# Decay sums as two float32r products, casts on ScalarE and a product on VectorE, in a fused RWKV-6 and max-out MLP kernel

## Chip, cores and metric

One core of one Trainium2 chip. The time is the device time of one execution in microseconds (us), given as the median of a kernel's runs. The profiled span is some 1.7 us shorter than the time of the same run. A run is called slow when it lies over 1.5% above the fastest of the same kernel; slow runs are left out of every ratio. A ratio is the mean time of one kernel's fast runs over that of the kernel before in the same rounds on the same chip, so it is not quite the ratio of the medians quoted beside it. Where two experiments are compared with each other, the difference of their ratios is taken, times 170.5 us (the median of the kernel before).

## The reference, cut to what matters

```python
# B=4 sequences, H=8 heads, S=768 steps, D=48; float32 in and out
state = 0
for t in range(S):                       # RWKV-6 recurrence
    y[t]  = r[t] @ (state + outer(u*k[t], v[t]))
    state = w[t][:, None]*state + outer(k[t], v[t])      # w in 0.80..0.95
x  = y as (3072 tokens, 384)
h1 = x @ w1;  h2 = x @ w2                # 384 x 1024 each
out = maximum(h1, h2) @ w_out            # 1024 x 384
```

The kernel works in 12 units: unit `i` is a chunk of 128 steps of two sequences. In a chunk the decay becomes a running sum of `ln w`, made on TensorE by a triangular matrix of ones (`ex`), and its exponentials scale r and k (`rp`, `kp`). The maximum is written as (h1+h2)/2 + |h1-h2|/2, so that the MLP needs one large product with w1-w2 (`H`, whose result is `g_p`) and one with half the sum of both already multiplied by w_out.

## The kernel before: the parts that matter

Every engine runs its instructions strictly in the order in which a long hand-made list, `ORDER`, names them. A token is an operation, a unit and at times a sequence: `ex.3.1` is the decay sum of unit 3, sequence 1. In the comments, SBUF and PSUM are the core's two on-chip memories; TensorE's results land in PSUM.

```python
ORDER = """
ldw.0 ldw.1 ldk.0 ldu ldr.0 ldw12.2 ldv.0 ldw12.0 lw.0 ex.0.0 incl.0.0 aex.0.0 ...
... Y.0.1 aex.1.1 incl.1.1 ldwo YO.0.1 row.1 ldv.1 ...        # some 900 tokens, cut
"""
...
def ldwo():                                           # w_out, on GpSimd's queue
    nc.gpsimd.dma_start(out=wo_sb, in_=moe_w_out.rearrange("(o p) n -> p o n", p=C))
def lw(i):                                            # ScalarE: ln w, float32
    x = work.tile([C, NB, H, D], F32, tag="lw", name="lw")
    nc.scalar.activation(x, st["w", i], AF.Ln)
def ex(i, b):                                         # TensorE: the decay sum, float32
    ex_p = ps.tile([C, HD], F32, tag="ex", name="ex_p")
    nc.tensor.matmul(ex_p, triU, flat(st["lw", i][:, b]))
def incl(i, b):                                       # VectorE
    nc.vector.tensor_add(flat(st["incl", i][:, b]), st["ex", i, b], flat(st["lw", i][:, b]))
def rp(i):                                            # VectorE, two SBUF inputs
    nc.vector.tensor_mul(rps[i % 2][:, :, :, 0:D], st["r", i], st["Aex", i])
def kp(i):                                            # VectorE, two SBUF inputs
    nc.vector.tensor_mul(kps[i % 2][:, :, :, 0:D], st["k", i], st["Ainv", i])
def ku(i):                                            # GpSimd: k*u
    nc.gpsimd.tensor_mul(x, st["k", i]..., u_b...)
def rku(i):                                           # GpSimd: k*u*r
    nc.gpsimd.tensor_mul(st["ku", i], st["r", i]..., st["ku", i])
def bv(i):                                            # GpSimd: v times the sum of k*u*r
    nc.gpsimd.tensor_mul(x..., st["v", i]..., st["dg", i]...)
def vb(i):                                            # GpSimd: v in bf16
    nc.gpsimd.tensor_copy(x, st["v", i])
def TO(i, b):                                         # transposed rp, kp out of PSUM
    if b == 0: nc.scalar.copy(rkT, st.pop(("tp", i, b)))
    else:      nc.vector.tensor_copy(rkT, st.pop(("tp", i, b)))
def sb(i):                                            # GpSimd: state in bf16
    for a in range(2): nc.gpsimd.tensor_copy(S_z[bp][rows, :, :, a, :], S_f[bp][rows])
...
with tc.manual_schedule():
    for step in ORDER.split():
        name, *at = step.split(".")
        ops[name](*(int(x) for x in at))
```

Of the kernel before, what the change touches and what calls it, by code (L numbers as in the profile page):

```python
# [8 lines left out]
F32 = mybir.dt.float32  # L9
BF16 = mybir.dt.bfloat16  # L10
# [6 lines left out]
ldw.0 ldw.1 ldk.0 ldu ldr.0 ldw12.2 ldv.0 ldw12.0 lw.0 ex.0.0 incl.0.0 aex.0.0 ex.0.1 incl.0.1 ainv.0 row.0  # L17
ldw.2 ldw12.1 ldr.1 ldk.1 ku.0 aex.0.1 kp.0 lw.1 ex.1.0 rp.0 rku.0 T.0.0 TO.0.0 wsum.2 aex.1.0 M.0.0 T.0.1
MO.0.0 TO.0.1 vb.0 dg.0 M.0.1 Y.0.0 wT.2 incl.1.0 bv.0 MO.0.1 ex.1.1 wdif.2 wsum.0 YO.0.0 lw.2 wdif.0 X.0.0
Y.0.1 aex.1.1 incl.1.1 ldwo YO.0.1 row.1 ldv.1 ldw.3 wt.0 wdif.1 ldk.2 X.0.1 ldr.2 wsum.1 ex.2.0 ldw.4 XO.0  # L20
wT.0 wTO.2 aex.2.0 ainv.1 wTO.0 H.0.0 incl.2.0 H.0.1 HO.0.0 rp.1 K.0 HO.0.1 H.0.2 kp.1 ku.1 wT.1 HO.0.2 ex.2.1
sa.0 T.1.0 wTO.1 H.0.3 rku.1 TO.1.0 incl.2.1 wp.0 wt.1 row.2 ldv.2 ldk.3 HO.0.3 ldr.3 T.1.1 wpO.0 dg.1 M.1.0
aex.2.1 vb.1 wp.2 MO.1.0 bv.1 K.1 wpO.2 wp.1 sa.1 lw.3 TO.1.1 ainv.2 Y.1.0 ex.3.0 YO.1.0 wpO.1 aex.3.0
incl.3.0 X.1.0 M.1.1 ku.2 wx.0 kp.2 O1.0.0 MO.1.1 O2.0.0 rku.2 ex.3.1 sm.0 OO.0.0 Y.1.1 rp.2 aex.3.1 O1.0.1
YO.1.1 sb.0 lw.4 T.2.0 incl.3.1 O2.0.1 dg.2 TO.2.0 row.3 ldw.5 wt.2 X.1.1 ldv.3 ex.4.0 ldr.4 ldk.4 ldw.6 XO.1
T.2.1 M.2.0 OO.0.1 bv.2 TO.2.1 H.1.0 aex.4.0 incl.4.0 H.1.1 HO.1.0 MO.2.0 ex.4.1 ainv.3 vb.2 H.1.2 HO.1.1 kp.3
wx.1 M.2.1 ku.3 HO.1.2 K.2 incl.4.1 Y.2.0 H.1.3 rp.3 wt.3 ldv.4 ldk.5 O1.1.0 row.4 st.0.0 HO.1.3 rku.3 ldr.5
YO.2.0 ainv.4 MO.2.1 T.3.0 O1.1.1 lw.5 sa.2 TO.3.0 sm.1 Y.2.1 dg.3 X.2.0 sb.1 O2.1.0 aex.4.1 T.3.1 YO.2.1
OO.1.0 M.3.0 TO.3.1 X.2.1 O2.1.1 vb.3 XO.2 MO.3.0 ex.5.0 OO.1.1 bv.3 H.2.0 wx.2 incl.5.0 aex.5.0 H.2.1 sm.2
HO.2.0 rp.4 ex.5.1 HO.2.1 ku.4 M.3.1 kp.4 aex.5.1 K.3 H.2.2 MO.3.1 H.2.3 HO.2.2 sb.2 T.4.0 Y.3.0 TO.4.0 O1.2.0  # L30
YO.3.0 sa.3 HO.2.3 Y.3.1 incl.5.1 vb.4 X.3.0 M.4.0 YO.3.1 row.5 ainv.5 st.0.1 T.4.1 ldv.5 ldw.7 MO.4.0 ldw.8
rku.4 ldr.6 ldk.6 O1.2.1 st.1.0 lw.6 kp.5 X.3.1 wt.4 O2.2.0 st.1.1 XO.3 ku.5 dg.4 O2.2.1 OO.2.0 ex.6.0 TO.4.1
Y.4.0 aex.6.0 incl.6.0 H.3.0 rp.5 rku.5 K.4 ex.6.1 sa.4 OO.2.1 T.5.0 incl.6.1 wx.3 HO.3.0 M.4.1 bv.4 H.3.1
TO.5.0 dg.5 row.6 ldv.6 wt.5 ldw.9 ldr.7 H.3.2 ldk.7 HO.3.1 MO.4.1 T.5.1 ainv.6 H.3.3 vb.5 sm.3 HO.3.2 M.5.0
YO.4.0 sb.3 K.5 lw.7 TO.5.1 O1.3.0 MO.5.0 aex.6.1 HO.3.3 Y.4.1 bv.5 ex.7.0 sa.5 lw.8 YO.4.1 M.5.1 O1.3.1
aex.7.0 incl.7.0 MO.5.1 Y.5.0 X.4.0 X.4.1 YO.5.0 ex.7.1 rp.6 O2.3.0 aex.7.1 XO.4 O2.3.1 incl.7.1 ku.6 kp.6
Y.5.1 OO.3.0 ex.8.0 row.7 wx.4 st.2.0 YO.5.1 st.2.1 ldk.8 H.4.0 ldv.7 ldr.8 rku.6 OO.3.1 T.6.0 incl.8.0 wt.6
st.3.0 HO.4.0 X.5.0 st.3.1 sm.4 H.4.1 TO.6.0 X.5.1 H.4.2 HO.4.1 dg.6 M.6.0 vb.6 HO.4.2 T.6.1 aex.8.0 MO.6.0
H.4.3 sb.4 XO.5 ex.8.1 HO.4.3 TO.6.1 H.5.0 incl.8.1 bv.6 H.5.1 HO.5.0 M.6.1 HO.5.1 H.5.2 MO.6.1 aex.8.1 Y.6.0
wx.5 HO.5.2 O1.4.0 ainv.7 YO.6.0 rp.7 lw.9 Y.6.1 O2.4.0 ku.7 kp.7 wt.7 ldw.10 ldv.8 ex.9.0 row.8 ldk.9 ldr.9  # L40
OO.4.0 sm.5 K.6 ainv.8 T.7.0 incl.9.0 st.4.0 rku.7 H.5.3 YO.6.1 TO.7.0 sa.6 O1.4.1 aex.9.0 HO.5.3 X.6.0 kp.8
sb.5 X.6.1 O2.4.1 XO.6 M.7.0 dg.7 OO.4.1 ex.9.1 ku.8 H.6.0 incl.9.1 H.6.1 MO.7.0 HO.6.0 T.7.1 aex.9.1 HO.6.1
H.6.2 vb.7 rp.8 H.6.3 HO.6.2 bv.7 Y.7.0 wx.6 TO.7.1 O1.5.0 wx.7 M.7.1 HO.6.3 rku.8 YO.7.0 K.7 T.8.0 MO.7.1
O1.5.1 TO.8.0 sm.6 O2.5.0 ainv.9 sa.7 sb.6 Y.7.1 sm.7 OO.5.0 X.7.0 M.8.0 YO.7.1 lw.10 T.8.1 dg.8 wt.8 O1.6.0
ldw.11 vb.8 ldk.10 ldv.9 ldr.10 row.9 st.4.1 TO.8.1 st.5.0 bv.8 X.7.1 MO.8.0 O2.5.1 XO.7 O2.6.0 OO.5.1 kp.9
M.8.1 st.5.1 sb.7 ex.10.0 Y.8.0 rp.9 H.7.0 K.8 ku.9 OO.6.0 incl.10.0 T.9.0 aex.10.0 YO.8.0 st.6.0 ldv.10 H.7.1
ldr.11 HO.7.0 ldk.11 MO.8.1 TO.9.0 ex.10.1 rku.9 H.7.2 HO.7.1 sa.8 Y.8.1 aex.10.1 M.9.0 HO.7.2 YO.8.1 T.9.1
incl.10.1 H.7.3 MO.9.0 ainv.10 X.8.0 X.8.1 O1.6.1 HO.7.3 kp.10 XO.8 O1.7.0 dg.9 vb.9 lw.11 O2.6.1 TO.9.1 bv.9
O2.7.0 rp.10 ex.11.0 M.9.1 incl.11.0 ku.10 K.9 OO.6.1 T.10.0 aex.11.0 st.6.1 ldv.11 Y.9.0 OO.7.0 H.8.0 TO.10.0
YO.9.0 st.7.0 wt.9 H.8.1 sa.9 rku.10 HO.8.0 MO.9.1 T.10.1 HO.8.1 H.8.2 TO.10.1 H.8.3 HO.8.2 ex.11.1 wx.8 vb.10  # L50
M.10.0 incl.11.1 aex.11.1 Y.9.1 dg.10 O1.7.1 ainv.11 YO.9.1 HO.8.3 bv.10 X.9.0 O2.7.1 rp.11 O1.8.0 OO.7.1 sm.8
st.7.1 kp.11 sb.8 X.9.1 O2.8.0 O1.8.1 MO.10.0 OO.8.0 XO.9 st.8.0 ku.11 T.11.0 M.10.1 TO.11.0 Y.10.0 MO.10.1
O2.8.1 rku.11 T.11.1 OO.8.1 YO.10.0 H.9.0 st.8.1 H.9.1 HO.9.0 Y.10.1 wx.9 HO.9.1 dg.11 H.9.2 X.10.0 YO.10.1
H.9.3 HO.9.2 bv.11 sm.9 M.11.0 HO.9.3 O1.9.0 MO.11.0 vb.11 O1.9.1 TO.11.1 sb.9 O2.9.0 X.10.1 M.11.1 OO.9.0
O2.9.1 XO.10 st.9.0 Y.11.0 OO.9.1 H.10.0 YO.11.0 st.9.1 H.10.1 MO.11.1 HO.10.0 X.11.0 HO.10.1 H.10.2 Y.11.1
HO.10.2 H.10.3 YO.11.1 O1.10.0 HO.10.3 X.11.1 O2.10.0 XO.11 O1.10.1 OO.10.0 st.10.0 O2.10.1 H.11.0 OO.10.1
st.10.1 H.11.1 HO.11.0 H.11.2 HO.11.1 H.11.3 HO.11.2 O1.11.0 HO.11.3 O2.11.0 O1.11.1 OO.11.0 st.11.0 O2.11.1
OO.11.1 st.11.1
# [4 lines left out]
def kernel(  # L63
# [12 lines left out]
    nc = tc.nc  # L76
# [25 lines left out]
    make_upper_triangular(nc, triU, val=1.0, diag=False)  # L102
    u_b = const.tile([C, HD], F32)

# [28 lines left out]
    w1f = const.tile([C, KO, d_ff], F32)  # L133
    w2f = const.tile([C, KO, d_ff], F32)

# [8 lines left out]


    def ldw12(ko):
        nc.sync.dma_start(out=w1f[:, ko, :], in_=moe_w1[ko * C:(ko + 1) * C, :])
        nc.sync.dma_start(out=w2f[:, ko, :], in_=moe_w2[ko * C:(ko + 1) * C, :])
# [7 lines left out]
    def wsum(ko):  # L156
        nc.gpsimd.tensor_add(ws_sb[:, ko, :], w1f[:, ko, :], w2f[:, ko, :])

    def wdif(ko):
        nc.vector.tensor_sub(wd_sb[:, ko, :], w1f[:, ko, :], w2f[:, ko, :])  # L160
# [21 lines left out]
    def ld(name, src):  # L182
        def fn(i):
            c, bp = units[i]
            x = inp.tile([C, NB, H, D], F32, tag=name, name=f"{name}t")
            nc.sync.dma_start(
                out=x, in_=src[bp * NB:(bp + 1) * NB, :, c * C:(c + 1) * C, :].rearrange("b h s d -> s b h d"))
            st[name, i] = x
        return fn

    def lw(i):
        x = work.tile([C, NB, H, D], F32, tag="lw", name="lw")
        nc.scalar.activation(x, st["w", i], AF.Ln)  # L193
        st["lw", i] = x

    def ex(i, b):
        ex_p = ps.tile([C, HD], F32, tag="ex", name="ex_p")
        nc.tensor.matmul(ex_p, triU, flat(st["lw", i][:, b]))  # L198
        st["ex", i, b] = ex_p
# [11 lines left out]
    def ainv(i):  # L211
        x = work.tile([C, NB, H, D], F32, tag="Ainv", name="Ainv")
        nc.scalar.activation(x, st["incl", i], AF.Exp, scale=-1.0)  # L213
        st["Ainv", i] = x
# [18 lines left out]
    def rp(i):  # L233
        nc.vector.tensor_mul(rps[i % 2][:, :, :, 0:D], st["r", i], st["Aex", i])  # L234

    def kp(i):
        nc.vector.tensor_mul(kps[i % 2][:, :, :, 0:D], st["k", i], st["Ainv", i])  # L237

    def ku(i):
        x = work.tile([C, NB, HD], F32, tag="ku", name="ku")  # L240
        nc.gpsimd.tensor_mul(x, st["k", i].rearrange("p b h d -> p b (h d)"),  # L241
                             u_b.unsqueeze(1).to_broadcast([C, NB, HD]))
        st["ku", i] = x

    def rku(i):
        nc.gpsimd.tensor_mul(st["ku", i], st["r", i].rearrange("p b h d -> p b (h d)"), st["ku", i])  # L246

    def dg(i):
        x = work.tile([C, NB * H, 1], F32, tag="dg", name="dg", bufs=3)
        nc.vector.reduce_sum(x, st["ku", i].rearrange("p b (h d) -> p (b h) d", d=D), axis=AX.X)  # L250
        st["dg", i] = x

    def bv(i):
        x = work.tile([C, NB, HD], F32, tag="bv", name="bv")
        nc.gpsimd.tensor_mul(x.rearrange("p b (h d) -> p (b h) d", d=D),  # L255
                             st["v", i].rearrange("p b h d -> p (b h) d"),
                             st["dg", i].to_broadcast([C, NB * H, D]))
        st["bv", i] = x
# [188 lines left out]
```

## Time and profile before

The kernel before takes 170.5 us. Its profile splits at the first block of `g_p`, which starts the MLP, and at the end of the last `xs`, VectorE's last long step. Three stretches result: the start, the dense stage, the tail.

| stage (us) | length | TensorE busy | VectorE busy | ScalarE busy | GpSimd busy |
|---|---|---|---|---|---|
| start, 4.5 to 32.9 | 28.40 | 14.37 | 19.72 | 7.99 | 19.90 |
| dense, 32.9 to 155.85 | 122.95 | 120.92 | 105.02 | 75.67 | 80.24 |
| tail, 155.85 to 169.8 | 13.95 | 10.42 | 0.05 | 5.60 | 0 |

In the dense stage TensorE stands idle for 2.0 us out of 123; it is the bound. The chain of work that ended last says the same (its line of shares, by engine):

```profile
PE 67%; DVE 18%; issue 5%; DMA 4%; ACT 4%; DVEq 0%; ACTq 0%
```

Two thirds of that chain are TensorE's own work. The prediction below shows the page's totals, the slices and the prices.

### The profile page before, as it was taken

The page shows a single profiled execution, that of the slowest core. Times are in us where ns is not written, and L with a number is a line of the kernel's source. Part 1 is how long each engine was busy: PE and PEld are TensorE (multiplying, and loading weights), DVE is VectorE, ACT ScalarE, POOL GpSimd, SP SyncE. Part 2 cuts the span into 40 slices and gives each one's busy share as a digit, 9 for nine tenths or more (in the row PEclk, how much of TensorE's full clock was granted, in tenths as well). Part 3 has the DMA queues.
Part 4 walks back from the last instruction along what each step waited for, and adds up shares of the span by engine and source line. Part 5 has one row for each costly group of instructions (what it writes and reads, how often), then busy time and mean ns, then how long its engine had stood idle before and what let it go on. Part 6 is the DMA issues. An engine that isn't in the chain of part 4 may idle for free.

```text
span 169.8 us, 3790 instructions
## 1 busy us (share of the span) xinstructions
PE 145.7 (86%) x1536; PEld 100.1 (59%) x1536; DVE 125.7 (74%) x148; ACT 90.6 (53%) x158; POOL 104.0 (61%) x86
## 2 busy tenths in 40 slices
PE   0435573599999989998999999999999999999991
PEld 0112442377557666775767776866776866867660
DVE  2146699955697999999989779999979698645000
ACT  3340321245647666573936888646584755635551
POOL 8159399924727929899394947918956838740000
PEclk9999999999999999999999999999999999999999
DMA  6999998999964999659979997999993702111112
GB/s 123 202 235 331 282 299 102 210 187 211 180 105 93 198 177 191 145 132 226 235 131 232 216 222 152 223 205 185 300 221 82 144 0 93 50 42 53 64 35 93
DMA packets 112614, 28.04 MB, mean 165 GB/s; under 512 B 107594, under 2 KB 111818, under 8 KB 112596
## 3 DMA queue, kind: packets, MB, share of 16 engines
q1 hardware_dynamic: 111556, 27.00, 75.4%
q0 software_dynamic: 1040, 0.79, 3.5%
q8 instruction: 12, 0.20, 0.5%
q14 instruction: 6, 0.05, 0.1%
HBM read 23.82 MB, written 4.75 MB: 168 GB/s over the span
## 4 chain that ended last, share of the span: by engine, by line
PE 67%; DVE 18%; issue 5%; DMA 4%; ACT 4%; DVEq 0%; ACTq 0%
PE o_p L378 17%; PE g_p L368 14%; PE ex_p L198 8%; PE tp L270 7%; PE o_p L384 6%; DVE rp L234 5%; PE mt_p L289 4%; DVE MTm L294 4%; PE y_p L305 2%; PE wc_p L174 2%; DVE wd_sb L160 2%; DMA wt<-in_w_dram 2%; PE xt_p L323 2%; DVE kp L237 2%; DMA Wt<-row 2%
## 5 line engine op out<-in xcount | busy, mean ns | idle before, releaser
L368 PE MATMUL g_p<-xT,wd_sb 128*128 128x256 bf16 x288 | 39.1, 282 | 2.1 <-DVE wsT_sb L169 2.1
L378 PE MATMUL o_p<-wo_sb,gT 128*128 128x384 bf16 x192 | 37.3, 326 | 0.0
L374 ACT ACTIVATE gT<-g_p 128x512 bf16<-128x512 f32 x48 | 28.6, 598 | 15.5 <-PE g_p L368 14.9
L294 DVE TENSOR_TENSOR MTm<-mt_p,triU 128x1024 bf16<-128x1024 f32 x24 | 29.2, 1215 | 7.1 <-PE mt_p L289 7.1
L368 PEld LDWEIGHTS <-wd_sb 128*128 128x128 bf16 x288 | 27.5, 100 | 8.6 <-DVE wsT_sb L169 2.3
L198 PE MATMUL ex_p<-lw,triU 128*128 128x384 f32 x48 | 24.3, 593 | 9.2 <-ACT lw L193 8.1
L255 POOL TENSOR_TENSOR bv<-vt,dg 128x768 f32<-128x768 f32 x12 | 17.7, 1473 | 15.7 <-DVE dg L250 11.2
L358 POOL CAST sz<-sf 48x384 bf16<-48x384 f32 x20 | 13.4, 672 | 22.0 <-DVE sf L351 21.4
L241 POOL TENSOR_TENSOR ku<-kt,u_b 128x768 f32<-128x768 f32 x12 | 23.0, 1920 | 5.7 <-DMA u_b<-in_u_dram 5.5
L246 POOL TENSOR_TENSOR ku<-rt,ku 128x768 f32<-128x768 f32 x12 | 24.4, 2034 | 0.8
L378 PEld LDWEIGHTS <-gT 128*128 128x128 bf16 x192 | 18.2, 98 | 11.2 <-issue 0.2
L204 DVE TENSOR_TENSOR incl<-ex_p,lw 128x384 f32<-128x384 f32 x24 | 13.2, 551 | 9.8 <-PE ex_p L198 8.3
L209 ACT ACTIVATE Aex<-ex_p 128x384 f32<-128x384 f32 x24 | 11.8, 491 | 14.3 <-DVE incl L204 7.4
L234 DVE TENSOR_TENSOR rp<-rt,Aex 128x768 bf16<-128x768 f32 x12 | 19.3, 1608 | 0.0
L393 ACT COPY osb<-o_p 128x384 f32<-128x384 f32 x24 | 11.5, 482 | 14.0 <-PE o_p L378 12.2
L278 ACT COPY rkT<-tp 128x1024 bf16<-128x1024 bf16 x12 | 12.2, 1013 | 12.7 <-PE tp L270 12.7
L316 DVE TENSOR_TENSOR xs<-y_p,bv 128x384 bf16<-128x384 f32 x24 | 13.2, 549 | 6.0 <-PE y_p L309 5.5
L237 DVE TENSOR_TENSOR kp<-kt,Ainv 128x768 bf16<-128x768 f32 x12 | 15.6, 1303 | 1.1 <-ACT Ainv L213 1.1
L198 PEld LDWEIGHTS ex_p<-lw,triU 128*128 128x128 f32 x48 | 8.6, 218 | 12.3 <-POOL sz L123 5.4
L384 PE MATMUL o_p<-wc_sb,xT 128*128 128x384 bf16 x72 | 15.7, 326 | 0.0
L327 ACT COPY xT<-xt_p 128x768 bf16<-128x768 bf16 x12 | 9.6, 800 | 8.2 <-PE xt_p L323 8.2
L262 POOL CAST vb<-vt 128x768 bf16<-128x768 f32 x12 | 12.6, 1046 | 1.6 <-DMA vt<-in_v_dram 1.4
(47 smaller groups left out, 199.9 us busy)
## 6 DMA issues: line engine op xcount, KB each, us to landing
wt<-in_w_dram SPq DMA_DIRECT2D x12, 384.0 KB, 4.9
kt<-in_k_dram SPq DMA_DIRECT2D x12, 384.0 KB, 5.7
rt<-in_r_dram SPq DMA_DIRECT2D x12, 384.0 KB, 5.1
vt<-in_v_dram SPq DMA_DIRECT2D x12, 384.0 KB, 5.1
out_dram<-osb SPq DMA_DIRECT2D x24, 192.0 KB, 2.6
w1f<-in_moe_w_dram SPq DMA_DIRECT2D x3, 512.0 KB, 7.0
w2f<-in_moe_w_dram SPq DMA_DIRECT2D x3, 512.0 KB, 4.8
wo_sb<-in_moe_w_out_dram POOLq DMA_DIRECT2D x1, 768.0 KB, 7.6
```

The costliest lines, as they stand in the source:

```text
L198: nc.tensor.matmul(ex_p, triU, flat(st["lw", i][:, b]))
L234: nc.vector.tensor_mul(rps[i % 2][:, :, :, 0:D], st["r", i], st["Aex", i])
L237: nc.vector.tensor_mul(kps[i % 2][:, :, :, 0:D], st["k", i], st["Ainv", i])
L241: nc.gpsimd.tensor_mul(x, st["k", i].rearrange("p b h d -> p b (h d)"), u_b.unsqueeze(1).to_broadcast([C, NB, HD]))
L246: nc.gpsimd.tensor_mul(st["ku", i], st["r", i].rearrange("p b h d -> p b (h d)"), st["ku", i])
L255: nc.gpsimd.tensor_mul(x.rearrange("p b (h d) -> p (b h) d", d=D), st["v", i].rearrange("p b h d -> p (b h) d"), st["dg", i].to_broadcast( ...
L294: nc.vector.tensor_mul(x.rearrange("p a q c -> p (a q) c"), st.pop(("mt", i, b)).rearrange("p a q c -> p (a q) c"), triU.unsqueeze(1).to_b ...
L358: nc.gpsimd.tensor_copy(S_z[bp][rows, :, :, a, :], S_f[bp][rows])
L368: nc.tensor.matmul(g_p[:, q, :], wd_sb[:, ko, fo * C:(fo + 1) * C], st["xT", i][:, ko].rearrange("p b c -> p (b c)"), start=(ko == 0), sto ...
L374: nc.scalar.activation(st["gT", i][:, f2 * 2:f2 * 2 + 2, :], st.pop(("g", i, f2)), AF.Abs, scale=0.5)
L378: nc.tensor.matmul(st["o", i, b], st["gT", i][:, fo, b * C:(b + 1) * C], wo_sb[:, fo, :], start=False, stop=(fo == FO - 1))
L384: nc.tensor.matmul(st["o", i, b], st["xT", i][:, ko, b, :], wc_sb[:, ko, :], start=(ko == 0), stop=False)
```

## The change

The intent: the float32 decay sum costs TensorE four bf16 passes. `ln w` is written twice, once rounded to float32r (`lwh`, high part) and once in float32; VectorE subtracts (`lwl`, low part), and two one-pass products add up. GpSimd is relieved: v's casts go to ScalarE and k*u*r to VectorE; in return ScalarE takes all copies of rkT. Idle products run while the first loads arrive.

```diff
+    triR = const.tile([C, C], F32R)
+    nc.gpsimd.tensor_copy(triR, triU)
+    def lwh(i, b=None):
+        nc.scalar.activation(new("lwh", i, b, F32R), get("w", i, b), AF.Ln)
+    def lwl(i, b=None):
+        nc.vector.tensor_sub(new("lwl", i, b, F32R), get("lw", i, b), get("lwh", i, b).bitcast(F32))
     def ex(i, b):
-        nc.tensor.matmul(ex_p, triU, flat(st["lw", i][:, b]))
+        nc.tensor.matmul(ex_p, triR, flat(st["lwh", i][:, b]), start=True, stop=False)
+        nc.tensor.matmul(ex_p, triR, flat(st["lwl", i][:, b]), start=False, stop=True)
     # rku:
-        nc.gpsimd.tensor_mul(st["ku", i], st["r", i]..., st["ku", i])
+        nc.vector.tensor_mul(rows_(get("ku", i, b)), rows_(get("r", i, b)), rows_(get("ku", i, b)))
     # vb:
-        nc.gpsimd.tensor_copy(x, st["v", i])
+        nc.scalar.copy(new("vb", i, b, BF16, 3), get("v", i, b))
     # TO: nc.scalar.copy for both sequences (before: VectorE for b == 1)
     # sb: nc.gpsimd.tensor_copy for a == 0, nc.scalar.copy for a == 1 (before: GpSimd for both)
+    def warm(tag): ...   # count products of 128x512 bf16 of zeros; 64 in all, all before H.0.0
     # w1, w2: a pool of two buffers per block (before: three standing tiles); xT: 6 buffers (before: 8)
     # unit 0 is loaded and worked through by sequence
     # ORDER: new throughout; in it ldwo stands behind ku.0.1, in the middle of the first loads
```

## The prediction

> **What bounds the kernel now.** I read, in this order, the page's engine totals and slices, busy time in windows, the groups by line, and the chain of work that ended last. Totals, then the 40 slices of 4.2 us:
>
> ```profile
> PE 145.7 (86%) x1536; PEld 100.1 (59%) x1536; DVE 125.7 (74%) x148; ACT 90.6 (53%) x158; POOL 104.0 (61%) x86
> ...
> PE   0435573599999989998999999999999999999991
> PEld 0112442377557666775767776866776866867660
> DVE  2146699955697999999989779999979698645000
> ```
>
> Two stages show. Up to slice 8 (about 33 us) TensorE is half idle; afterwards it is at 9 nearly throughout, so TensorE bounds the rest. VectorE is close behind in the middle. Windows (stretch, length, then busy us of PE, PEld, DVE, ACT, POOL, clock, DMA share, GB/s):
>
> ```profile
> 20.00:25.00 5.00, 3.92 (x37) 2.59 (x37) 5.00 (x7) 1.33 (x2) 3.81 (x2) 1.00 1.01 287
> 25.00:30.00 5.00, 2.07 (x12) 1.15 (x10) 5.00 (x4) 0.80 (x1) 4.98 (x4) 1.00 0.87 120
> 30.00:35.00 5.00, 2.93 (x18) 2.08 (x17) 5.00 (x6) 1.80 (x3) 3.85 (x2) 1.00 1.28 221
> ...
> 60.00:70.00 10.00, 9.78 (x113) 6.96 (x113) 10.00 (x13) 6.22 (x12) 6.56 (x7) 1.00 1.04 202
> ```
>
> From 20 to 35 us VectorE is full while TensorE works 8.9 of 15 us: VectorE sets when the first block of the MLP (L368) starts, at 32.9 us. From 60 to 70 both are full. Summing such rows, TensorE idles 18.5 us before 35 us, about 2 from 35 to 155, and 3.5 in the last ten. Prices from the chain (start, us, what):
>
> ```profile
> 5.43 1.63 PE ex_p L198 x2
> ...
> 95.54 0.66 PE g_p L368 x6
> 96.20 0.65 PE ex_p L198 x2
> ...
> 140.12 0.65 PE o_p L378 x4
> ```
>
> One decay sum of 384 columns costs 1.63 us early and 0.65 later. Four bf16 products of 384 columns cost 0.65, so 0.163 each: the float32 sum is four bf16 products long.
>
> **What the Trainium skill says.** (1) "FP8 and Floating Point Precision", TensorE Precision Notes: true FP32 takes four passes, and a reduced form reads 4-byte FP32 and truncates it. The trace agrees on the four (0.65 against 0.163); no run here yet shows the reduced one. (2) "TensorE: Matmul & The Clock Gate", Part 1: an idle array runs at half clock until it has been busy some 3.4 us. The 1.63 against 0.65 agrees in direction, though the recorded clock reads 1.00 in every window. (3) Same page, Weight-path perf modes: fast weight load is not for FP32. The mean weight load is 218 ns at L198 and 98 to 102 ns for bf16. (4) "SBUF — State Buffer", Who interferes with whom: a VectorE instruction with two SBUF inputs and a GpSimd instruction that reads SBUF exclude each other for whole instructions. It agrees:
>
> ```profile
> 103.76 1.81 POOL L241 TENSOR_TENSOR ku<-kt,u_b 128x768 f32<-128x768 f32 x1
> 103.86 2.52 DVE L237 TENSOR_TENSOR kp<-kt,Ainv 128x768 bf16<-128x768 f32 x1
> ```
>
> The product that takes 0.945 us at best took 2.52: it stood until GpSimd ended at 105.57.
>
> **TensorE.** Each decay sum becomes two one-pass products, 2 x 0.163 = 0.33 us; with 0.2 us weight loads that may not hide I take 0.39. The group falls from 24.3 us (its row, x48) to 24 x 0.39 = 9.4. Of the 15 us, five cold sums lose about 6 where TensorE waits anyway; 19 sums in the dense stage lose 0.26 each, 5 us. The new order also does ex.2.1 and both sums of unit 3 ahead of that stage, 3 x 0.65 = 2 us more. 64 idle products go in, all ahead of the first MLP block; they cost nothing if they end before the data they stand in front of, and should make the first real products run warm.
>
> **VectorE.** Means and minima are from the groups and the listings of single lines.
>
> ```profile
> L234 DVE TENSOR_TENSOR rp<-rt,Aex 128x768 bf16<-128x768 f32 x12 | 19.3, 1608 | 0.0
> L237 DVE TENSOR_TENSOR kp<-kt,Ainv 128x768 bf16<-128x768 f32 x12 | 15.6, 1303 | 1.1 <-ACT Ainv L213 1.1
> L280 DVE COPY rkT<-tp 128x1024 bf16<-128x1024 bf16 x12 | 8.2, 680 | 0.9 <-PE tp L270 0.9
> ```
>
> Lost to the port today: rp 12 x (1.608 - 0.942) = 8.0, kp 12 x (1.303 - 0.945) = 4.3, the state product 10 x (0.806 - 0.542) = 2.6, the weight differences 3 x (2.801 - 1.215) = 4.8; together 19.7 of 125.7. Without it: 106.0. The change takes 12 copies of rkT away (-7.4 net of the 0.06 us by which neighbours overlap) and adds lwl and k*u*r, both of the form of kp: 24 units of 0.945 less overlap, +21.4. Splitting unit 0 into sequences adds some 0.7. Base after: 120.7. Now the port. Before, 37 such instructions lost 0.53 us each with GpSimd reading about 92 us of 160. After, there are 65 (13 lwl, 13 k*u*r, 13 rp, 13 kp, 10 state, 3 weights), but GpSimd reads only 12 x 1.81 (ku) + 12 x 1.47 (bv) + 10 x 0.53 (sz) + 3 x 2.4 (ws) = 52 us. In proportion 0.53 x 52/92 = 0.30 each, 65 x 0.30 = 19; a schedule that avoids some gives 15. I take 17: VectorE then needs about **138 us**, 12 more than now.
>
> **ScalarE and GpSimd.** ScalarE gains a second Ln (10.1 us, as L193), casts of v (12 x 0.8), the other 12 copies of rkT (12 x 1.01) and half of sz (10 x 0.48): 90.6 + 37 = 128. GpSimd falls from 104 to about 60.
>
> **Start.** The first load is half as large: w is in at 4.4 us now, say 3.7 after. Two half Ln (0.49 each, as the 384-column L209), lwl 0.54 (as the fastest L351) and the sum 0.5 make it available near 6, against 7.05 (5.43 + 1.62). The gate on the MLP is the third pair of weights, for every block of g_p sums over all three: counted along the queue of loads in the new order, 5.5 MB lie up to its end, and the loads moved 1.6 MB by 10 us and 4.5 more by 25, so it lands near 23. But VectorE has 18.7 us of base work ahead of that last difference, plus 4 for the port, from 4.7 us on: 27.4. First block at 27 to 28 rather than 32.9, **5 us** gained.
>
> **Sum, two ways.** By TensorE: 122.5 us lie between 33 and 155.5; less 5 and 2 gives 115, so 27.5 + 115 + 14 (tail) = 156.5, if nothing else bounds. By VectorE: it starts near 4.7 with 1 us of fill instructions behind it; 137 us of work and 5 idle (4%; in the before it worked 66 of the 70 us from 50 to 120, when TensorE was the bound) end near 147; after its last xs come the transposes, O of unit 10, H and O of unit 11, a copy and a store: 0.2 + 3.6 + 2.6 + 3.6 plus some 3 = 13. That is 160. The later one decides: **VectorE becomes the bound**, and I put the time at 160.5 us.
>
> **Rivals.** (a) TensorE stays the bound and the gain is whole, 154 to 157. For: 40 us leave GpSimd's reading (92 to 52), each VectorE product then waits less for the port, and the new order may have been laid around it. Against: 37 us go to ScalarE and 15 to VectorE even without such waits. (b) The moved work eats the gain: three engines at 80 to 88% in strict order, with only two buffers for g_p and o_p, so that ScalarE's copies come late. For: ScalarE's share rises from 53% to 80%. It makes 165 to 170. (c) The one-pass product is not at bf16 speed, or its unhidden weight load makes a sum 0.65 again: 5 us of TensorE come back, but mostly under VectorE, so 162 to 164. (d) The first loads are what bounds the start anyway, or the ten idle products (cold, some 4 us) delay the first sum: the 5 us shrink to 2, hence 163.
>
> **Range and chances.** The two sums give 156.5 and 160; rival (a) reaches down to 154, (b) up to 170. The port's 15 to 22 us and an idle share of 2 to 8% each move the end by 3 to 5 us. Hence 155 to 166.5. Over 2% faster means under 167.1, which only (b) at its worst misses: 0.90. Within 2%: 0.08. Slower: 0.02.
>
> **What would show it.** Right: ex_p 24 x 0.33 to 0.45 us with two records each; no cold sum above 0.6; VectorE 134 to 143 us and above 85% of the span, in nearly all middle slices at 9; rp, kp, lwl, k*u*r with means of 1.1 to 1.4 us; the first L368-type block at 26 to 29 us; TensorE's slices at 7 to 9 instead of 9, with waits on VectorE first in the list. Wrong: ex_p at 0.6 (c); VectorE below 130 with TensorE full (a); waits for ScalarE's gT, rkT or vb foremost (b); or the first block after 31 us (d).

## The result, and the profile after

The changed kernel takes 183.79 us in the median (181.54 to 184.43) against 170.5; the ratio is 1.0719, with a 95% interval of 1.063 to 1.0808. It is slower, and correct. The profiled run is the fastest of them (181.54 us, mean granted TensorE clock 0.981; the other four have 0.953 and 182.97 to 184.43 us), so the profile understates the loss a little. First the totals and four rows of slices (4.5 us each) of the changed kernel:

```profile
PE 152.2 (85%) x1600; PEld 103.3 (57%) x1600; DVE 137.8 (77%) x166; ACT 124.2 (69%) x208; POOL 62.0 (34%) x55
...
PE   6996709859977996699987999699799799999992
...
DVE  2557905997999999579979998979899998962000
...
PEclk9999996999999999889999999999999999999999
```

The demands came as predicted: VectorE 137.8 us (138 was said), ScalarE 124.2 (128), GpSimd 62.0 (60). But neither row is full. TensorE's has sixes and sevens all through, and VectorE's has holes too. The dense stage in windows (columns: stretch, length, busy us of PE, PEld, DVE, ACT, POOL, clock, DMA share, GB/s), before:

```profile
32.90:155.85 122.95, 120.92 (x1386) 85.79 (x1387) 105.02 (x130) 75.67 (x135) 80.24 (x63) 1.00 0.81 162
```

and after:

```profile
35.00:165.05 130.05, 115.53 (x1362) 83.74 (x1361) 117.58 (x137) 103.41 (x175) 42.56 (x32) 0.99 0.73 149
```

TensorE does have 5.4 us less to do there, but the stage is 7.1 us longer: its idle time went from 2.0 to 14.5 us. VectorE is busy for 90%. No engine is full; they wait for each other. The chain that ended last, after:

```profile
PE 38%; DVE 34%; ACT 7%; DMA 7%; SPq 7%; issue 5%; ACTq 0%; DVEq 0%
```

Where two thirds were TensorE's, now TensorE and VectorE share it, and 14% are a transfer and its issue. One such hand-over in the dense stage of the changed kernel, from its timeline (start, us, engine, line, what; in brackets the idle time before and what ended it):

```profile
68.84 2.52 POOL L280 TENSOR_TENSOR ku<-kt,u_b 128x768 f32<-128x768 f32 x1
...
69.63 2.55 DVE L273 TENSOR_TENSOR kp<-kt,Ainv 128x768 bf16<-128x768 f32 x1
...
72.10 0.55 DVE L242 TENSOR_TENSOR incl<-ex_p,lw 128x384 f32<-128x384 f32 x1
...
72.74 0.49 ACT L247 ACTIVATE Aex<-ex_p 128x384 f32<-128x384 f32 x1 [3.57 <-DVE incl L242]
73.13 0.47 ACT L423 COPY osb<-o_p 128x384 f32<-128x384 f32 x1
...
73.65 0.82 PE L398 MATMUL g_p<-xT,wd_sb 128*128 128x256 bf16 x6 [3.29 <-ACT osb L423]
```

Read it downwards. "The port" is short for what these lines and the prediction's show: a VectorE product with two SBUF inputs stands while a GpSimd instruction that reads SBUF is under way. `kp` takes 0.95 us when undisturbed; here it stands until GpSimd's `ku` ends at 71.36. `incl` stands behind it, ScalarE's `Aex` waits 3.57 us for `incl`, the copy `osb` waits behind `Aex` in ScalarE's order, and TensorE waits 3.29 us for the buffer that `osb` frees. So a wait of 1.6 us for the port holds up three engines one after the other; by these durations it makes about half of TensorE's 3.29 us. It can be worse; in the same kernel a VectorE product waited behind two GpSimd instructions in a row, 3.03 us for 0.55 us of work:

```profile
112.92 1.80 POOL L280 TENSOR_TENSOR ku<-kt,u_b 128x768 f32<-128x768 f32 x1
113.54 3.03 DVE L381 TENSOR_TENSOR sf<-sf,Wx 128x384 f32<-128x384 f32 x1
...
114.69 1.46 POOL L293 TENSOR_TENSOR bv<-vt,dg 128x768 f32<-128x768 f32 x1
```

The start went wrong in another way. The first `g_p` block of the changed kernel starts at 35.0 us, not at 27.5. Issues and the first use of v in its timeline:

```profile
13.80 4.20 SPq L218 DMA_DIRECT2D vt<-in_v_dram  x1
...
16.63 1.05 POOL L182 DMA_DIRECT2D wo_sb<-in_moe_w_out_dram  x1
...
26.72 0.51 ACT L296 CAST vb<-vt 128x384 bf16<-128x384 f32 x1 [4.94 <-DMA vt<-in_v_dram]
```

and the load of w_out in the kernel before:

```profile
25.98 1.05 POOL L151 DMA_DIRECT2D wo_sb<-in_moe_w_out_dram  x1
```

The load of w_out (1024 x 384 float32, 1.57 MB) moved ahead from 26.0 to 16.6 us, on its own queue, into the busiest time of the loads. v, issued at 13.80, lands only at 26.72, and everything behind it waits.

### The profile page after: what moved, and what is told of

It reads as the page before. It is cut to its first block, busy times and chain, and to the rows that moved or that the text cites. A ratio compares the mean times of both kernels' runs of the same rounds, so it can differ in the third digit from the quotient of the medians.

```text
span 179.8 us, 3964 instructions
## 1 busy us (share of the span) xinstructions
PE 152.2 (85%) x1600; PEld 103.3 (57%) x1600; DVE 137.8 (77%) x166; ACT 124.2 (69%) x208; POOL 62.0 (34%) x55
## 4 chain that ended last, share of the span: by engine, by line
PE 38%; DVE 34%; ACT 7%; DMA 7%; SPq 7%; issue 5%; ACTq 0%; DVEq 0%
PE g_p L398 12%; PE o_p L408 9%; DMA vt<-in_v_dram 7%; SPq L218 5%; DVE MTm L324 5%; DVE rp L270 4%; DVE kp L273 4%; DVE sf L381 4%; DVE ku L284 4%; PE o_p L414 3%; DVE xs L346 3%; DVE lwl L231 3%; PE tp L303 3%; DVE dg L289 3%; DVE incl L242 2%
## 5 line engine op out<-in xcount | busy, mean ns | idle before, releaser
L398 PE MATMUL g_p<-xT,wd_sb 128*128 128x256 bf16 x288 | 37.7, 276 | 4.2 <-ACT osb L423 3.3
L293 POOL TENSOR_TENSOR bv<-vt,dg 128x768 f32<-128x768 f32 (+1 forms) x13 | 18.8, 1448 | 40.4 <-DVE dg L289 18.7
L280 POOL TENSOR_TENSOR ku<-kt,u_b 128x768 f32<-128x768 f32 (+1 forms) x13 | 23.0, 1771 | 16.6 <-DMA kt<-in_k_dram 8.9
L310 ACT COPY rkT<-tp 128x1024 bf16<-128x1024 bf16 x24 | 24.3, 1012 | 5.2 <-PE tp L303 5.2
L231 DVE TENSOR_TENSOR lwl<-lw,lwh 128x768 fp32r<-128x768 f32 (+1 forms) x13 | 15.1, 1162 | 10.0 <-ACT lwh L228 6.9
L171 PE MATMUL warm<-blank,ident 128*128 128x512 bf16 x64 | 19.0, 435 | 1.5 <-POOL ident masks.py:199 1.5
L388 POOL CAST sz<-sf 48x384 bf16<-48x384 f32 x10 | 6.8, 684 | 34.5 <-DVE sf L381 34.5
L423 ACT COPY osb<-o_p 128x384 f32<-128x384 f32 x24 | 11.5, 479 | 7.9 <-PE o_p L408 5.5
L273 DVE TENSOR_TENSOR kp<-kt,Ainv 128x768 bf16<-128x768 f32 (+1 forms) x13 | 15.5, 1193 | 0.0
L270 DVE TENSOR_TENSOR rp<-rt,Aex 128x768 bf16<-128x768 f32 (+1 forms) x13 | 15.1, 1162 | 0.0
L335 PE MATMUL y_p<-vb,MTm 128*128 128x48 bf16 x192 | 9.0, 186 | 6.5 <-ACT vb L296 5.4
L284 DVE TENSOR_TENSOR ku<-rt,ku 128x768 f32<-128x768 f32 (+1 forms) x13 | 13.7, 1052 | 0.1
```

Of the source, the lines that this page charges most:

```text
L171: nc.tensor.matmul(x, ident, blank)
L231: nc.vector.tensor_sub(new("lwl", i, b, F32R), get("lw", i, b), get("lwh", i, b).bitcast(F32))
L270: nc.vector.tensor_mul(rps[i % 2][:, seqs(b), :, 0:D], get("r", i, b), get("Aex", i, b))
L273: nc.vector.tensor_mul(kps[i % 2][:, seqs(b), :, 0:D], get("k", i, b), get("Ainv", i, b))
L280: nc.gpsimd.tensor_mul(rows_(x), rows_(get("k", i, b)), u_b.unsqueeze(1).to_broadcast([C, x.shape[1], HD]))
L284: nc.vector.tensor_mul(rows_(get("ku", i, b)), rows_(get("r", i, b)), rows_(get("ku", i, b)))
```

## The experiments

The theories, in words. The VectorE theory: its added work is the loss, with or without waits. The port theory: VectorE's new products stand behind GpSimd, and in the strict order these waits stop the other engines. The start theory: the early w_out load delays v. The order theory: the new order is worse by itself. The ScalarE theory: its new work comes late. The low-part theory: TensorE waits for `lwl`. The expectations are quoted as they were written before each run; where they name a theory by a letter, V is VectorE's work, P the port, S the start, O the order, A ScalarE and D the wait for `lwl`. Below, "the changed kernel" is the one measured above; the base of most is `p1_wo_late`.

| run | median us | ratio to the kernel before | 95% interval |
|---|---|---|---|
| changed kernel | 183.79 | 1.0719 | 1.063 to 1.0808 |
| p1_wo_late | 180.35 | 1.0531 | 1.0469 to 1.0594 |
| p3_v_early_wo_late | 182.74 | 1.0657 | 1.0606 to 1.0708 |
| o1_new_order_old_ops | 181.53 | 1.0632 | 1.0602 to 1.0663 |
| o2_old_order_new_ops | 195.08 | 1.1409 | 1.1389 to 1.1429 |
| q1_rku_pool | 180.76 | 1.0582 | 1.0529 to 1.0635 |
| q2_one_pass | 171.67 | 1.0065 | 1.0009 to 1.0121 |
| q3_no_split | 175.97 | 1.0329 | 1.0287 to 1.037 |
| q4_port_off (wrong) | 167.66 | 0.9855 | 0.9795 to 0.9916 |
| b1_before_port_off (wrong) | 163.59 | 0.9593 | 0.956 to 0.9627 |
| v2_before_split | 191.12 | none: 3 of 4 runs slow | |
| v3_before_rku_vector | 168.50 | 0.9786 (2 of 4 runs slow) | 0.9735 to 0.9838 |
| v4_before_scalar | 170.57 | 0.9991 | 0.9933 to 1.0048 |
| d1_low_unread (wrong) | 180.34 | 1.0556 | 1.0489 to 1.0623 |
| d2_low_tiny | 174.68 | 1.0204 | 1.0139 to 1.027 |
| n1_no_idle | 181.10 | 1.0605 | 1.0538 to 1.0673 |
| v5_before_one_pass_rku | 164.25 | 0.9636 | 0.9578 to 0.9694 |
| e1_port_off_low_tiny (wrong) | 166.34 | 0.9769 | 0.9733 to 0.9804 |
| v6_before_one_pass_rku_act | 166.10 | 0.9746 | 0.9712 to 0.978 |

### Start: p1_wo_late and p3_v_early_wo_late

p1 is the changed kernel with the w_out load later. p3 also moves the loads of v of unit 0 ahead of the first MLP weights.

```diff
 # ORDER, p1:
-... ldr.1 ku.0.1 ldwo wsum.1 ...   ... incl.2.0 wsum.2 ldk.2 ...
+... ldr.1 ku.0.1 wsum.1 ...        ... incl.2.0 wsum.2 ldwo ldk.2 ...
 # ORDER, p3, in addition: ldv.0.0 ldv.0.1 before ldw12.0
```

> The changed kernel with one edit: the load of w_out (1.5 MB read, on the GpSimd queue) goes back behind the third weight sum, as in the kernel before. Theory S (start): in the changed kernel v of unit 0 landed at 26.7 us, because w_out moved up to 16.6 us and shares the DMA engines with it. If that is right, v lands 3 to 5 us earlier (22 to 24), the first MLP block moves from 35.0 to 31 to 33, and the time falls by 2 to 4 us to about 180. Theory V (VectorE): only VectorE's load in the dense stage matters; then the start moves but the time stays within 1 us of 183.8. Theory O (order): no change beyond 1 us.

> As the run before, and v of unit 0 is also put ahead of the first pair of weights in the queue of loads. Theory S: v lands at 12 to 14 us, nothing on the way to the first MLP block waits for it, the block starts at 27 to 30 us, and the time falls 5 to 7 us, to 177 to 179. Theory V: VectorE does the same work and the dense stage is as long as before, so an earlier start is kept whole only if VectorE's work also moves forward; it has 11.6 idle us between 4.5 and 35, so up to 6 us can be gained here too. Theory O: under 2 us.

In p1 the first cast of v starts at 21.3 us instead of 26.7, and the first `g_p` block at 29.4 us, 5.6 earlier. The whole gains 1.9% (3.2 us): the dense stage is longer by 2.6 us.

```profile
29.40:162.05 132.65, 117.99 (x1361) 85.11 (x1361) 114.18 (x137) 103.85 (x175) 45.57 (x33) 0.96 0.79 155
```

That is the dense stage of p1 in the same columns: TensorE idles 14.7 us of it. p3 started the block at 31.1 and was slower than p1: there VectorE waits 3.2 us rather than 1.5 for the weights that were moved back, and v is cast only at 23.7.

The edit of p1 has a price of its own. The load of w_out is now issued at 28.8 us and lands at 37.7, and the new order asks for it (`wc_p`, w_out times the sum of w1 and w2) at 35.3. The group `wc_p` in the kernel before, in p1 and in q4 below, which is built on p1 (columns: busy us, mean ns of one, idle before and its releaser):

```profile
L174 PE MATMUL wc_p<-wo_sb,wsT_sb 128*128 128x384 bf16 x24 | 4.4, 327 | 0.0
L205 PE MATMUL wc_p<-wo_sb,wsT_sb 128*128 128x384 bf16 x24 | 6.7, 445 | 2.4 <-DMA wo_sb<-in_moe_w_out_dram 2.4
L205 PE MATMUL wc_p<-wo_sb,wsT_sb 128*128 128x384 bf16 x24 | 5.7, 392 | 3.8 <-DMA wo_sb<-in_moe_w_out_dram 3.8
```

TensorE stands still for this load, 1.0 to 3.8 us, in p1 and in every kernel built on it but n1, and in p1 and q4 its clock falls with it (see e1 below). The start theory thus holds for a quarter of the loss as p1 shows it; a load placed between the two was not tried and may be worth more.

### Order against operations: o1_new_order_old_ops and o2_old_order_new_ops

o1 is the changed kernel with all operations as before: float32 sums, k*u*r, casts and state copies on their old engines, no idle products (`lwh`, `lwl` and `warm` tokens removed). It keeps the early w_out load and the split of unit 0. o2 is the changed kernel's operations in the old order. It needed fewer buffers to fit (w 3 instead of 4, `lwl` 1 instead of 2), w1 and w2 in three, and one `lwl` token placed later.

> The new order and the split unit 0, but every operation on its old engine: float32 decay sums, casts of v and k*u*r on GpSimd, every second copy of rkT on VectorE, both halves of the state cast on GpSimd, no idle products. Theory O (the new order loses by itself): about as slow as the changed kernel, 180 to 186. Theory V (moved work): VectorE drops to some 120 us busy and the time goes to 172 to 176, the rest being the start. If the order was made for the new engines, an order unfit for the old ones may also give over 186; that would speak for neither.

> The old order with all the new operations on their new engines (the added Ln and subtraction right beside the old Ln, no idle products; w in three buffers and the low parts in one, so that it fits). Theory V: the moved work alone loses, so this is slower than before, 175 to 182, with VectorE at 136 us or more and full from 35 to 130. Theory O: the operations are good and the new order bad, so this is at 162 to 168. Theory S: near 170, for the old queue of loads is back.

The new order alone, with the old operations, costs 6.3% (10.8 us), nearly the whole loss; its dense stage is 129.45 us long with TensorE busy for 120.72. The new operations in the old order cost 14%, partly through the smaller buffers. So the parts do not add: each order fits its own operations at best, and the new one, even with its own, is behind the old one with the old. The order theory is right that the order is not free, but o1 alone does not say why.

### The port: q4_port_off, b1_before_port_off, q1_rku_pool

In q4, GpSimd's `ku`, `bv` and half of `sz` of p1 read one column only, and write the rest as constants, so that GpSimd stays as busy (64.1 us over the whole, against p1's 62.5) but hardly reads SBUF. The result is wrong. b1 does the same to the kernel before, for `ku`, `rku`, `bv`, `vb` and `sz`.

```diff
 # q4, ku (bv and sb alike)
-        nc.gpsimd.tensor_mul(rows_(x), rows_(get("k", i, b)), u_b...)
+        y = rows_(x)
+        nc.gpsimd.tensor_mul(y[:, :, 0:1], rows_(get("k", i, b))[:, :, 0:1], u_b[:, 0:1]...)
+        for _ in range(2):
+            nc.gpsimd.memset(y[:, :, 1:], 0.01)
 # q1, on p1
-        nc.vector.tensor_mul(rows_(get("ku", i, b)), ...)
+        nc.gpsimd.tensor_mul(rows_(get("ku", i, b)), ...)
```

> As the late load of w_out, but GpSimd's ku, bv and its half of the state cast read one column and otherwise only write constants, for about the same time (wrong result on purpose; loads, sums and buffers are still waited for). Theory P: VectorE's products stop waiting (lwl, rp, kp and k*u*r at 0.95 us for 768 columns, the state product at 0.55), VectorE falls by 15 to 18 us busy to some 118, and the time falls by 8 to 12 us, to 168 to 172. Theory V in its plain form (the work itself, not the waits): 3 us at most. Theory A or O: 3 us at most.

> The kernel before, with GpSimd's ku, k*u*r, bv, casts of v and state casts reading one column and otherwise writing constants for about the same time (wrong result on purpose), as was done to the changed kernel, where it took 12.7 us off. Theory P (the waits for the shared read port lie on the path in the changed kernel and did not before, for TensorE was the bound): VectorE's rp, kp and state products fall to 0.95 and 0.55 us, VectorE loses some 15 us busy, and the time falls by only 0 to 4 us. If the port costs the kernel before as much (8 us or more), then it is not what the change added, and theory O stands.

> The kernel with the late load of w_out (180.4 us) with one more edit: the product k*u*r goes back to GpSimd. Theory V (VectorE's added work is the loss): VectorE loses 13.7 us of its group and gains some port waits, ends near 125 us busy, and the time falls by 5 to 8 us, to 172 to 175. Theory P (the port: VectorE products with two SBUF inputs wait behind GpSimd instructions, and the waits lie on the path): GpSimd reads 22 us more, each of the 52 other such products waits longer, the two cancel, and the time stays within 2 us. Theory O (the order fits neither): slower, as the dg sums now wait for GpSimd.

Two groups of VectorE in the changed kernel (columns: busy us, mean ns of one, idle before and its releasers):

```profile
L231 DVE TENSOR_TENSOR lwl<-lw,lwh 128x768 fp32r<-128x768 f32 (+1 forms) x13 | 15.1, 1162 | 10.0 <-ACT lwh L228 6.9 <-ACT lw L224 3.1
...
L273 DVE TENSOR_TENSOR kp<-kt,Ainv 128x768 bf16<-128x768 f32 (+1 forms) x13 | 15.5, 1193 | 0.0
```

and in q4:

```profile
L231 DVE TENSOR_TENSOR lwl<-lw,lwh 128x768 fp32r<-128x768 f32 (+1 forms) x13 | 11.6, 895 | 6.1 <-ACT lw L224 3.7 <-ACT lwh L228 2.3
...
L273 DVE TENSOR_TENSOR kp<-kt,Ainv 128x768 bf16<-128x768 f32 (+1 forms) x13 | 11.5, 888 | 0.0
```

The work is the same and GpSimd as busy; only its reading is gone, and each of these takes 0.3 us less. VectorE's total is 121.0 us (p1: 135.1), the prediction's "base after" of 120.7. The whole gains 6.8% of the time before (11.5 us) on p1, with VectorE's work untouched, so the VectorE theory in its plain form falls. In the kernel before the same edit gains 4.1% (6.9 us). So the port costs both kernels, and the changed one 4.6 us more. My theory that the port was the changed kernel's problem only falls. The dense stages of q4 and b1, with the port off in both:

```profile
28.40:151.25 122.85, 114.30 (x1363) 83.51 (x1362) 101.75 (x137) 103.13 (x175) 45.91 (x87) 0.99 0.84 167
29.70:147.75 118.05, 117.98 (x1386) 84.67 (x1387) 93.23 (x130) 75.74 (x136) 75.19 (x160) 1.00 0.86 173
```

TensorE is idle for 8.6 us of q4's stage and for 0.1 of b1's. The largest piece of the 8.6 is the wait of 3.8 us for w_out shown above, which b1 does not have. q1 moves k*u*r back to GpSimd: VectorE has 13 instructions fewer, but `kp` goes from a mean of 1.01 us in p1 to 1.59, VectorE's total only from 135.1 to 134.1, and the time stays within its interval. Less work on VectorE and more reading on GpSimd cancel.

### The decay sum: q2_one_pass, q3_no_split, d1_low_unread, d2_low_tiny

All on p1. q2 uses a single float32r product of one rounded `ln w`; q3 a float32 product as before; neither has `lwh` or `lwl`. d1 still computes `lwl`, but the second product reads the high part again, so TensorE does not wait for VectorE. d2 keeps that wait but lets VectorE subtract one column only, into two standing tiles.

```diff
 # q2: lw is written as float32r
+        nc.tensor.matmul(ex_p, triR, flat(st["lw", i][:, b]))
 # q3
+        nc.tensor.matmul(ex_p, triU, flat(st["lw", i][:, b]))
 # d1
-        nc.tensor.matmul(ex_p, triR, flat(st["lwl", i][:, b]), start=False, stop=True)
+        nc.tensor.matmul(ex_p, triR, flat(st["lwh", i][:, b]), start=False, stop=True)
 # d2
+        st["lwl", i] = lows[i % 2]
-        nc.vector.tensor_sub(new("lwl", i, b, F32R), ...)
+        nc.vector.tensor_sub(get("lwl", i, b)[:, :, 0, 0:1], ...)
```

> As the late load of w_out, but the decay sum is a single float32r product of one rounded Ln: no second Ln on ScalarE (-10 us), no subtraction on VectorE (-15 us), TensorE as cheap as it gets. Less exact than the reference on purpose. Theory V: this is the largest cut in VectorE's work, so the time falls by 6 to 10 us, to 170 to 174. Theory P: 13 of the 65 exposed products are gone, a fifth, so 2 to 4 us. Theory A (ScalarE's strict order holds back its copies out of PSUM): 10 of 124 us on ScalarE gone, 2 to 4 us.

> As the late load of w_out, with the decay sums in float32 again, as in the kernel before: no second Ln and no subtraction, but some 0.3 us more of TensorE for each of 24 sums. Beside the one-product kernel it tells what the cheap product itself is worth: if TensorE bounds the dense stage the difference is 6 to 7 us, if VectorE or ScalarE do it is under 2. Against the late load alone: theory V 4 to 8 us faster, since VectorE loses 15 us of work for 7 us more on TensorE; if the high and low parts are a net gain, slower by 3 or more.

> The kernel with the late load of w_out (180.4 us) with the second product reading the high part again (wrong result on purpose): VectorE still makes the low part, ScalarE still makes both Ln, TensorE still runs two products, but no decay sum waits for VectorE. Theory D (the new wait of TensorE on VectorE is the loss): 174 to 177. Theories V and P (the low part's time on VectorE and its place at the port): within 2 us of 180.4.

> The same kernel with the wait kept and the work taken away: VectorE's subtraction covers one column in each sequence of a standing tile (wrong result on purpose), and the product reads that tile whole. VectorE loses some 13 us, of which 3.6 are port waits. Theories V and P: 174 to 177. Theory D: within 2 us of 180.4. If this and the run before each take off 2 to 4 us, both count; if neither does, the second Ln on ScalarE is left as the cause.

q3 against p1: the split as a whole loses 2.0% (3.4 us) against the float32 product that it replaces. q2 against q3: a cheaper product alone, without its low part, wins 2.6% (4.5 us), about the 5 us that I had taken for the dense stage. d1 changes nothing: TensorE's wait for `lwl` is not the cause, and the low-part theory falls. d2 wins 3.3% (5.6 us): it is VectorE's work for the low part that costs. q2 and d2 pass the check against the reference, so that the low part is below its tolerance on these data.

What TensorE paid for two products, from its timeline of the changed kernel:

```profile
79.56 0.42 PE L235 MATMUL ex_p<-lwh,triR 128*128 128x384 f32 x1
79.82 0.34 PE L236 MATMUL ex_p<-lwl,triR 128*128 128x384 f32 x1
80.09 0.40 PE L319 MATMUL mt_p<-rkT 48*128 48x128 bf16 x8
```

The granted clock is 1.00 here. From start to start 0.26 and 0.27 us: 0.53 for a sum, not 0.39. It is cheaper than 0.65, but by less than half of what was counted.

### The low part without the port: e1_port_off_low_tiny

p1 with the edits of q4 and d2 together.

> The kernel with the late load of w_out, with both edits that paid: GpSimd does not read (167.7 us alone) and VectorE's subtraction is one column (174.7 alone); wrong result on purpose. If the rest of the loss is the low part's plain work on VectorE, the time falls by 3 to 5 us more, to 163 to 165, no worse than the kernel before with the port off (163.6). If TensorE and ScalarE bound what is left, it stays at 166.5 to 168.

Only 0.9% (1.5 us) below q4, where the same edit won 5.6 us with the port on. This fits a low part that is dear mainly because it is one more VectorE product with two SBUF inputs: it waits for GpSimd, and the others queue behind it. It is not shown alone: without the port's waits VectorE is busy for only 83% of q4's dense stage (101.75 of 122.85), and q4 and e1 share the wait of 3.7 to 3.8 us for w_out, so any work taken off VectorE may count for less there. The dense stage of e1:

```profile
28.50:149.15 120.65, 114.19 (x1361) 83.51 (x1361) 94.82 (x137) 103.13 (x175) 44.13 (x87) 0.99 0.86 170
```

Compare its TensorE column with p1's: the same 1361 products take 114.19 us here and 117.99 there. Up to 3.8 us of the cost of waiting is thus not standing still, but products that run slower. The granted clock, the third number from the right, accounts for it: it is 0.96 in p1 and 0.99 in e1, and busy time times clock is about 113 us in both. In p1 it reads 0.50 from 37 to 43 us and 0.58 from 71 to 75, around and after pauses of TensorE of 2.4 us (for w_out) and 2.8 us (for `osb`); in e1 it reads 0.50 from 36 to 39 us, after the w_out wait, and 1.00 from 69 to 75; in the kernel before it is 1.00 in all three stages. In the changed kernel it reads 0.50 from 75 to 78 us, after the pause at 70.4 to 73.65, and a float32r product at 74.72, as the clock fell, was recorded with 0.66 us instead of 0.42. That such a pause lowers the clock is a reading of these traces; no run tests it, and not every pause shows it: in o1 TensorE waits 4.8 us for `vb` and the clock reads 1.00 throughout. Nor does the column show every slow product: early float32 sums take 1.65 us there under a recorded 1.00.

### Other parts: n1_no_idle, v3_before_rku_vector, v4_before_scalar, v2_before_split

n1 is p1 without the idle products. The others add one part of the change to the kernel before, in its old order: v3 k*u*r on VectorE; v4 the casts of v and all copies of rkT on ScalarE; v2 the split alone (with w 3, xT 6 and `lwl` 1 buffers, to fit).

```diff
 # n1: all warm_* tokens removed from ORDER
 # v3, rku:  nc.gpsimd.tensor_mul -> nc.vector.tensor_mul
 # v4, vb:   nc.gpsimd.tensor_copy -> nc.scalar.copy;  TO: nc.scalar.copy for both sequences
 # v2: lwh, lwl and ex as in the change
```

> The kernel with the late load of w_out without its 64 idle products. If they pay, the first products run at half speed again (records of 0.8 us and more for float32r sums, transposes at 1.05 us for eight) and the time rises by 1 to 3 us. If they stand in the way (they hold the buffers of xt, mt and y and fill TensorE's queue), it falls by up to 2. If the start is bound by loads and VectorE: within 1 us.

> The kernel before with k*u*r alone moved from GpSimd to VectorE. VectorE gains 12 x 1.1 = 13 us, GpSimd loses 24 and holds the port less. Theory V: 173 to 178. Theory P: the fewer readings pay for the exposed products, 169 to 173. Theory O, on how finely an order fits its operations: any single move costs 3 us or more.

> The kernel before with the two moves to ScalarE alone: casts of v from GpSimd and every second copy of rkT from VectorE. ScalarE gains 22 us (91 to 113), VectorE loses 8 and GpSimd 12. Theory A (a fuller ScalarE in strict order delays its copies out of PSUM): 3 to 8 us slower. Theories V and P: both of VectorE's loads fall, so 0 to 3 us faster.

> The kernel before with the decay sums alone changed: a second, rounded Ln on ScalarE, the low part on VectorE, two float32r products (w in three buffers, low part and the transposed x in fewer, so that it fits). Theory V/P: VectorE gains 12 products exposed to a GpSimd that still reads 92 us, 12 x 1.3 = 16 us more, and the time rises to 174 to 182 although TensorE loses 7 us. If the split pays by itself: 163 to 168.

The idle products neither help nor hurt that the intervals could show; the first block starts at 29.6 us without and 29.4 with them, although the early products then run visibly colder (8 transposes of the weights in 1.06 us rather than 0.61). The comparison is not quite clean, for n1 is the one kernel of this family that does not wait for w_out. k*u*r on VectorE is probably a gain in the old order: 2.1% from its two fast runs, 1.5% if all four are counted (the two called slow have the full clock); the verdict by rule is unclear. ScalarE's added work is neutral there: the ScalarE theory does not explain the loss in the old order. v2 settles nothing: three of its four runs count as slow, and its smaller buffers delay the first block to 38.8 us.

### Putting the good parts together: v5 and v6

v5 is the kernel before, with its old order, one float32r product per sum and k*u*r on VectorE. v6 adds v4's two moves.

```diff
 # v5
-        x = work.tile([C, NB, H, D], F32, tag="lw", name="lw")
+        x = work.tile([C, NB, H, D], F32R, tag="lw", name="lw")
-        nc.tensor.matmul(ex_p, triU, flat(st["lw", i][:, b]))
+        nc.tensor.matmul(ex_p, triR, flat(st["lw", i][:, b]))
-        nc.gpsimd.tensor_mul(st["ku", i], ...)
+        nc.vector.tensor_mul(st["ku", i], ...)
```

> The kernel before in its old order with two edits: the decay sum as a single float32r product of one Ln (no low part; it stayed within the tolerance in the new order), and k*u*r on VectorE, which alone gave 2%. TensorE loses 7 us in a kernel that it bounds. If the old order's dense stage is bound by TensorE: 160 to 164. If VectorE, at 131 us busy with k*u*r, bounds it: 166 to 168, nothing gained over k*u*r alone.

> The old order with the single float32r product and k*u*r on VectorE (164.3 us), and also the casts of v and all copies of rkT on ScalarE. VectorE loses 8 us of 129, GpSimd 12 of reading. If VectorE with its port waits bounds that kernel now: 160 to 163. If TensorE still does (113 of 120 us busy in the dense stage): 163 to 165. If ScalarE's strict order costs: over 165.

v5 is correct, and with 164.25 us faster than both kernels. Its dense stage:

```profile
28.50:148.25 119.75, 113.13 (x1367) 82.33 (x1368) 110.68 (x141) 75.01 (x135) 62.06 (x53) 1.00 0.86 170
```

VectorE is busy for 92% and TensorE for 94% at once; 119.75 us is 10.3 less than in the changed kernel. v6 gives back 1.1% (1.9 us): once TensorE is cheaper, the moves to ScalarE do cost. The ScalarE theory is right by that much here (1.1% with an interval of some 0.7% either way).

## Why the prediction was wrong

Right were the demands, and with them the working behind them: VectorE's total (137.8 against 138) and its base without the port (121.0 in q4 against 120.7). The port's loss of busy time, put at 17 us, is 16.8 by these two, but 14.1 between p1 (135.1) and q4, the pair that differs in nothing else. Right too were ScalarE's and GpSimd's totals and the first decay sum near 6 us (6.5 measured). Right in direction was that VectorE and the port, not TensorE, set the pace: rival (a) is refuted.

The step that failed is "137 us of work and 5 idle (4%...)". The prediction added 4.7 + 1 + 137 + 5 + 13. The profile gives, in the same terms, 4.5 before the start, VectorE busy 18.95 + 117.58 us up to the last `xs`, idle 11.55 in the start and 12.47 in the dense stage, and a tail of 14.75: 179.8. Idle is 24.0 us where 5 were said, and this term alone makes 19 of the 19.3 us by which the span of 179.8 lies over 160.5. (The median time lies 23.3 us over: the sum was one of spans and left out the 1.7 us outside the span, and the profiled run is 2.3 us faster than the median.) VectorE was then busy for 77% of the span, where above 85% had been named as the sign of being right. The idle time has two parts.

In the start (11.55 us idle) the failed input was "5.5 MB lie up to its end", the count of loads ahead of the third pair of weights. It followed SyncE's queue and left out w_out, which goes out on GpSimd's queue and had moved from 26.0 to 16.6 us. The gate was another than forecast, too: the chain of the changed kernel's start runs through v (12.9 us from issue to landing), not through the third pair of weights. Even in p1, without w_out in the way, that pair lands at 26.4 us and not near 23. That the loads bound the start was rival (d), which I had put at 2 to 3 us. p1 shows 3.2 us for that load, after the new wait for it that p1 brings in.

In the dense stage (12.47 us idle) the assumption was that an engine that becomes the bound is kept fed at 96%. The figure was leaned on a stretch of the kernel before in which VectorE happened to work 66 of 70 us, which is 94%, and would have made 8 us of idle time; over that kernel's whole dense stage it is 105.02 of 122.95, 85%, in the windows above. The first hand-over shown above is how it went instead: with three engines at 80 to 90% in a strict order, a wait for the port is not only VectorE's loss: ScalarE and TensorE stop with it, and then VectorE waits for them. This was rival (b), with the port rather than ScalarE as what starts the waits.

The loss of 7.2% (12.3 us) divides by the ratios as follows: 1.9% (3.2 us) for the early load, from the changed kernel to p1; 2.7% (4.6 us) for the port's extra cost, 6.8% in p1 less 4.1% in the kernel before; and 2.6% (4.5 us) which remains between q4 and b1, with the port off in both. This last part is there although the sums are cheaper and q4's first block is earlier (28.4 us against 29.7). The traces name a candidate that is not in the changed kernel at all: q4's wait of 3.8 us for w_out and the clock of 0.50 from 36 to 39 us after it, which come with p1's place for that load and which b1 does not have. If they are the cause, these 4.5 us belong to the start, that is, to where the load stands, more than to the moved work; no run removes them. v6 against v5 shows that ScalarE's moves can cost 1.9 us, in the old order. How much of the rest lies in how the new order places the work is open: o1 shows that the order by itself loses 10.8 us with the old operations, which includes the early load, and apart from w_out and v no run separates one placement from another. Each ratio has an interval of 0.3 to 0.9% either way, so these parts are good to 1 to 2 us.

Smaller: a decay sum costs 0.53 us, not 0.39, so TensorE's saving in the dense stage was 0.12 and not 0.26 a sum; under the VectorE waits that cost little. The group's 15 us of saving was also too high by the prediction's own prices (5 x 1.63 + 19 x 0.65 is 20.5 us, not the row's 24.3); the sum did not use it.

## What to carry to other kernels

Before work is moved to an engine that shares a port with a second one, count the port's waits as waits of all engines that follow in order, not as busy time of one. What such a wait costs depends on what stands behind it: GpSimd's reading cost VectorE 15.8 us of busy time in the kernel before (125.7 to 109.9) and 14.1 in p1, and was worth 6.9 us of the end in the first and 11.5 in the second. Do not take the idle share of a new bound from a good stretch: take it over the whole stage. When a load is moved ahead, recount what lies before every other early load, on all queues together; and when it is moved back, look for who now waits for it: the first edit of the experiments cured one wait of 4.9 us (for v) and made another of 2.4 (for w_out).

## What the Trainium skill lacked or had wrong

- "SBUF — State Buffer", Who interferes with whom: the exclusion is confirmed; that a product can be kept waiting behind two instructions in a row is not on the page: a 0.55 us VectorE product took 3.03 us behind two of GpSimd's, and taking GpSimd's reading away was worth 6.9 us of 170.5 in one kernel and 11.5 in the other.
- "FP8 and Floating Point Precision", TensorE Precision Notes: it gives no rate for the reduced form. If float32r is that form, which no page states, then here a float32r product of 384 columns took 0.26 to 0.27 us from start to start, between bf16 (0.163) and float32 (0.65).
- No page that I read tells what idle products ahead of the data are worth: 64 of them changed neither the first block (29.4 and 29.6 us) nor the time by more than the intervals.
- Nor what a tuned order is worth with other operations than its own: the new one with the old operations took 181.53 us, the old one with the new operations (and fewer buffers) 195.08, where the kernel before took 170.5.
